# Block-sorted attention with a gated MLP: half of the first q by another queue, spatial weights turned in pairs, single output tiles, and a new order of units

## The chip, the cores and the metric

The kernel runs on one core of a Trainium2 chip. The metric is the device time of one execution in microseconds (us), the median of several runs. A profiled execution stands beside them: its span runs from the first to the last instruction of the core, and its own time is a little longer than the span.

## What is computed

The inputs are q, k and v (batch 4, 8 heads, 768 tokens, head size 64), an 8 x 8 matrix `sort_net` for each batch and head, and the weights of the MLP. All are fp32, and so is the output, 4 x 768 x 512. Cut to what matters:

```python
P = sort_net
for _ in range(5):                       # Sinkhorn rounds
    P = exp(P - max(P, -1)); P = P / sum(P, -1); P = P / sum(P, -2)
k_sorted = einsum('bhij,bhjcd->bhicd', P, k_blocks)      # 8 blocks of 96 tokens
v_sorted = einsum('bhij,bhjcd->bhicd', P, v_blocks)
attn = softmax(q_block @ k_sorted_block.T / 8)           # within each block
x = (attn @ v_sorted_block) as [batch, token, 512]
h = relu(x @ w_in);  u, v = h[..., :512], h[..., 512:]
v_n = (v - mean(v)) / sqrt(var(v) + 1e-6)                # over the 512 features
v_s = einsum('ts,bsd->btd', w_spatial, v_n) + b_spatial  # over the 768 tokens
out = (u * v_s) @ w_out
```

## The kernel before, in words

The work is written as units, short functions named by two letters. The string ORDER (lines 18 to 50) lists 355 of them by hand; the loop at line 755 calls them one after the other. No scheduler moves anything: each engine (and each engine's DMA queue) gets its instructions in the order in which the units issue them, and starts each one as soon as those before it on that engine have started and what it needs is there. In an item such as `SC:1:0:3:0` the first number of a unit that uses TensorE is the PSUM tile (four tiles of two banks, `ps0` to `ps3`); a letter A, D or P names ScalarE, VectorE or GpSimd; then come batch, head pair (four per batch) or tile, and half.

**Preamble.** `S0` loads sort_net by SyncE (L183). `SK:0` to `SK:4` (L224) are the Sinkhorn rounds: an exp on ScalarE (L232), then six short VectorE steps, strictly one after the other. `ID` makes the identity matrix on GpSimd, `MC` (L210) spreads it over 512 columns, `MA` and `MB` (L204, L207) make a mask. `DM` units (L217) are dummy matmuls on zeros. `PR` (L247) brings the Sinkhorn result to all partitions; `P0` (L261) multiplies it with the mask into the sorting matrices of batch 0 on VectorE, `PC` (L270) copies it to SBUF for `PD` (L273), which does the same for the other batches on GpSimd.

**Loads.** `L` (L157) issues all big loads on GpSimd's DMA queue, which casts from fp32 to bf16 on the way. q, k and v of a batch take one `ld` slot of 768 KB each. There are eight such slots, used in turn by q, k, v, the two halves of w_spatial and, later, the output tiles; a load waits until its slot is free. In order of issue: q0, k0, v0, v1, k1, q1, w_in's v half (`wv`), its u half (`wu`), the first half of w_spatial (`wsa`), and so on.

**Attention of a batch.** `QT` (one head pair, L312) and `QQ` (two, L318) turn q on TensorE (L308) and copy it out of PSUM. `KT` (L371) multiplies k with the sorting matrix. For batch 0, `VT` and `VB` (L374, L377) do the same for v. For batches 1 to 3, `VM` (L387) sorts v for all heads, and `VC` (L401, the DMA at L404) lets SyncE's queue copy each of the eight blocks of 96 tokens into `vb`, where `IV` has set a column of ones (L215). `SC` (L415) makes the scores and their exp (L428); `AT` (L460) multiplies with v and divides by the sum on VectorE (L476, L477). `XT` (L492) turns the result on TensorE; for batches 2 and 3 `XD` (L483) does it by a transposing DMA of SyncE's queue.

**MLP of a batch.** `VP` (L528, matmuls L535) is the v half of the first projection, with its relu; `ST`, `LN`, `LA` (L546 to L568) normalise on VectorE and ScalarE; `UP` (L570) is the u half (L578). `WT` (L502) turns one of the six 128-row strips of w_spatial (six transposes and one 768-wide copy). `SP` (L585) multiplies with the spatial weights and adds the bias, `GT` (L602) multiplies with u on GpSimd or VectorE. `OP` (L609) makes two output tiles of 128 tokens at once (eight matmuls, L616), `OE` (L623) copies them out of PSUM, and `OS` (L629) stores them by SyncE's queue. For the last batch there are finer units: `SH` and `GH` (L641, L654) work on tokens 0 to 511 or 512 to 767, and `OH`, `OI`, `OJ` (L661, L671, L676) make, copy and store one output tile or half of one.

`CK` and `CF` (L680, L695) test that sums stayed in range, `LF` (L701) loads the flag into all engines; the general path behind the branch at L759 is not taken.

Of the kernel before, what the change touches and what calls it, by code (L numbers as in the profile page):

```python
# [23 lines left out]
VM:3:A:1:3 AT:2:0:0:0 IV:1 VB:0:D:0:3 L:v:3:0:8 SC:1:0:3:0 VC:1:4:8 AT:2:0:2:0 SC:3:0:2:1 AT:0:0:3:0 BI SC:1:0:3:1
KT:2:A:1:3 AT:3:0:0:1 XT:1:A:0:0:2 AT:0:0:3:1 XT:2:A:0:0:0 XT:3:D:0:1:0 VC:1:0:4 KT:1:A:1:1 QQ:0:D:1:2 KT:2:A:1:0
PD:2:4:8 KT:3:A:1:2 QQ:1:A:1:0 AT:0:0:2:1 VP:2:D:0:0:1 SC:3:1:3:1 XT:0:D:0:1:2 VP:1:D:0:2 SC:3:1:0:1 ST:0:2 ST:0:0
SC:2:1:1:0 VP:0:A:0:4:5 VP:1:A:0:3 ST:0:1 ST:0:5 ST:0:3 SC:3:1:1:1 ST:0:4 SC:2:1:2:1 UP:0:A:0:1:0 UP:3:A:0:0:1
AT:1:1:1:1 L:k:3:0:8 AT:2:1:3:1 LN:0:0:6 PD:3:4:8 L:q:3:0:8 PD:3:0:4 UP:0:A:0:1:1 LA:0:1 AT:1:1:0:1 LA:0:0
UP:3:A:0:0:0 LA:0:5 WT:2:A:0 LA:0:2 WT:0:D:5 LA:0:3 WT:1:A:1 WT:3:D:4 WT:0:D:2 SC:2:1:3:0 AT:3:1:2:1 VM:1:A:2:1
WT:0:D:3 LA:0:4 VM:2:A:2:3 SC:3:1:0:0 VM:1:A:2:0 VM:0:D:2:2 VC:2:4:8 SP:2:0:3 AT:3:1:1:0 VC:2:0:4 AT:0:1:3:0 GT:D:0:3  # L30
SP:1:0:1 SP:2:0:2 SC:0:1:2:0 AT:1:1:0:0 KT:3:A:2:3 GT:P:0:2 XT:2:A:1:1:2 KT:0:D:2:1 KT:3:A:2:0 QQ:1:D:2:0 GT:P:0:1
QQ:2:D:2:2 KT:0:A:2:2 AT:3:1:2:0 SP:1:0:0 SC:3:2:0:0 XT:0:D:1:1:0 XT:2:A:1:0:0 XT:1:D:1:0:2 AT:3:2:0:0 SC:0:2:1:0
VM:2:A:3:2 VP:1:A:1:2:3 GT:P:0:0 VM:0:A:3:3 AT:2:2:1:0 ST:1:3 VP:3:D:1:4:5 VM:0:A:3:0 VM:2:D:3:1 VP:1:A:1:0:1
SC:0:2:3:0 SC:2:2:0:1 ST:1:5 OP:3:0:2 ST:1:0 ST:1:4 OE:A:0:2 VC:3:4:8 ST:1:2 SC:0:2:3:1 SC:1:2:1:1 UP:2:A:1:1:0
UP:3:A:1:0:1 VC:3:0:4 ST:1:1 AT:1:2:3:0 UP:0:D:1:0:0 LN:1:0:6 LA:1:3 LA:1:1 SC:3:2:2:1 SC:1:2:2:0 OP:2:0:0 KT:1:D:3:1
OE:A:0:0 KT:3:A:3:2 QQ:0:A:3:2 OS:0:2 LA:1:2 AT:2:2:2:0 LA:1:5 LA:1:0 LA:1:4 AT:1:2:3:1 OP:3:0:4 XD:2:0 AT:0:2:0:1
OE:A:0:4 UP:2:A:1:1:1 AT:3:2:1:1 AT:1:2:2:1 XD:2:1 SP:0:1:0 SC:1:3:2:0 QQ:2:D:3:0 KT:3:D:3:3 GT:P:1:0 KT:0:A:3:0
VP:1:D:2:0:1 SC:2:3:0:1 SC:3:3:1:0 VP:0:A:2:4:5 AT:3:3:2:0 AT:1:3:0:1 ST:2:4 SP:2:1:2 ST:2:1 ST:2:0 GT:P:1:2
SC:3:3:0:0 SC:1:3:3:1 VP:0:A:2:2:3 AT:2:3:1:0 ST:2:2 SP:1:1:3 SC:2:3:3:0 ST:2:5 GT:P:1:3 SC:0:3:2:1 SP:3:1:1 ST:2:3
SC:0:3:1:1 AT:2:3:0:0 UP:1:A:2:1:1 AT:0:3:3:0 LN:2:0:6 GT:P:1:1 UP:3:A:2:0:1 UP:1:A:2:1:0 LA:2:1 AT:2:3:3:1 AT:0:3:1:1  # L40
OP:3:1:2 AT:2:3:2:1 LA:2:3 OE:A:1:2 LA:2:2 UP:0:A:2:0:0 OP:2:1:0 LA:2:5 LA:2:0 OP:0:1:4 XD:3:0 XD:3:1 LA:2:4 OE:A:1:4
CK OE:D:1:0 SP:3:2:3 GT:P:2:3 CF:0 SP:2:2:2 VP:0:A:3:0:1 VP:1:D:3:2:3 VP:3:A:3:4:5 ST:3:2 ST:3:5 OS:0:4 SP:2:2:0
ST:3:1 SP:3:2:1 GT:P:2:0 UP:0:A:3:0:1 GT:D:2:2 ST:3:3 UP:2:A:3:0:0 UP:3:A:3:1:0 ST:3:4 ST:3:0 LN:3:0:6 LF LA:3:0
# [21 lines left out]
def kernel(  # L65
# [38 lines left out]
    def ps_tile(n, dt=FP32):  # L104
        return psum.tile([128, 2, 512 if dt == FP32 else 1024], dt, name=f"ps{n}", tag=f"ps{n}")

    def copy(eng, out, in_):
        if eng == "A":
            nc.scalar.copy(out=out, in_=in_)  # L109
# [39 lines left out]
    st = {}  # L149
    count = {"e": 0, "k": 0}  # L150

    def ld_tile(name):
# [55 lines left out]
        nc.vector.tensor_copy(out=mask16, in_=m32)  # L208

    def u_MC():  # L210
        nc.vector.tensor_copy(out=spread, in_=ident[0:BH, 0:BH].to_broadcast([BH, BH, TB]))
# [579 lines left out]
```

## Time and profile before

| | |
|---|---|
| median of 3 runs | 161.76 us (161.35 to 162.33) |
| the profiled execution | 162.01 us |
| its span | 160.1 us, mean granted TensorE clock 0.985 |
| DMA, bytes | GpSimd's queue 12.19 MB, SyncE's queue 10.70 MB |
| exp of the scores, L428, ScalarE | 32 of 810 ns, 24.5 us |
| spatial matmuls, L590 | 144 of 326 ns, 25.1 us |

Busy times are sums of instruction durations with overlaps counted once; matmuls are pipelined, so a matmul of 326 ns starts well before the one ahead of it has ended. "Granted clock" is the share of TensorE's full clock that it was given. SPq and POOLq are the sequencers of SyncE and GpSimd as issuers of DMAs. In a group row, the part behind the last bar is the time in which the engine stood idle before these instructions, with what ended it.

### The profile page before, as it was taken

Reading aid. Unit: us, or ns where it says so; the run is one execution under the profiler, and the core shown is the slowest. Engines: PE = TensorE matmul, PEld = TensorE weight load, DVE = VectorE, ACT = ScalarE, POOL = GpSimd, SP = SyncE. Lnnn points to the kernel's source line nnn. Section 1 sums busy time; section 2 is a strip of 40 time slices with the busy share of each in tenths; the row PEclk is TensorE's granted clock in tenths of the full one; section 3 lists DMA queues with packets and bytes.
Section 4 is the critical chain, followed back from the end, with each engine's and each line's share of the span. In section 5 each row is a group of like instructions: output and inputs, shape, how many; then the busy total and the mean of one; then the engine's idle time right before and its main releaser. Section 6 shows DMA issues by size and latency. Waiting matters only on the chain.

```text
span 160.1 us, 3999 instructions
## 1 busy us (share of the span) xinstructions
...
## 2 busy tenths in 40 slices
...
GB/s 14 184 204 205 204 205 204 207 217 249 264 206 205 213 248 220 204 130 108 184 49 98 100 5 0 0 4 98 122 107 209 57 0 0 0 330 327 39 315 55
DMA packets 27526, 23.19 MB, mean 145 GB/s; under 512 B 7280, under 2 KB 24432, under 8 KB 27504
## 3 DMA queue, kind: packets, MB, share of 16 engines
q0 software_dynamic: 14864, 12.19, 48.5%
q1 hardware_dynamic: 12640, 10.70, 23.7%
...
## 4 chain that ended last, share of the span: by engine, by line
PE 76%; DVE 8%; ACT 6%; DMA 4%; issue 1%
PE ps L590 14%; PE ps L578 13%; PE ps L535 12%; PE ps L616 12%; PE ps L646 5%; PE ps L469 4%; PE ps L423 3%; PE ps L364 3%; DMA xT<-x_sb 3%; PE ps L391 2%; PE ps L499 2%; ACT kt L109 2%; PE ps L308 2%; ACT ex L428 2%; DVE x_sb L477 2%; PE ps L505 1%
## 5 line engine op out<-in xcount | busy, mean ns | idle before, releaser
L606 POOL TENSOR_TENSOR gt<-z,u_sb 128x768 bf16<-128x768 f32 x10 | 17.0, 1706 | 76.1 <-ACT ex L428 42.2
L428 ACT ACTIVATE ex<-ps 96x768 bf16<-96x768 f32 x32 | 24.5, 810 | 18.0 <-PE ps L423 17.9
L590 PE MATMUL ps<-wspT,v_sb 128*128 128x384 bf16 x144 | 25.1, 326 | 0.0
L535 PE MATMUL ps<-w_in_sb,xT 128*128 128x512 bf16 x96 | 22.4, 379 | 0.9 <-ACT kt L109 0.8
L477 DVE TENSOR_TENSOR x_sb<-ps,rec_all 96x512 bf16<-96x512 f32 x32 | 22.0, 686 | 1.1
L578 PE MATMUL ps<-xT,w_in_sb 128*128 128x384 bf16 x128 | 22.6, 326 | 0.0
L616 PE MATMUL ps<-w_out_sb,gt 128*128 128x512 bf16 x88 | 20.2, 379 | 0.0
L109 ACT COPY o_sb<-ps 128x1024 f32<-128x1024 f32 (+1 forms) x9 | 8.4, 943 | 20.5 <-PE ps L616 19.8
L590 PEld LDWEIGHTS <-v_sb 128*128 128x128 bf16 x144 | 13.6, 98 | 8.7
L552 DVE BATCH_NORM_STATS2 stats<-v_sb 128x6 f32<-128x512 bf16 x24 | 16.2, 676 | 1.3 <-ACT v_sb L115 1.1
L115 ACT ACTIVATE u_sb<-ps 128x768 bf16<-128x768 f32 x14 | 11.4, 814 | 9.6 <-PE ps L578 9.5
L578 PEld LDWEIGHTS <-w_in_sb 128*128 128x128 bf16 x128 | 11.8, 98 | 7.4
L596 DVE TENSOR_TENSOR z<-ps,b_bc 128x768 f32<-128x768 f32 x12 | 11.5, 955 | 5.5 <-PE ps L590 4.0
L535 PEld LDWEIGHTS <-xT 128*128 128x128 bf16 x96 | 8.9, 98 | 10.8 <-issue 0.9
L616 PEld LDWEIGHTS <-gt 128*128 128x128 bf16 x88 | 8.3, 98 | 9.2
L115 ACT ACTIVATE v_sb<-ps 128x1024 bf16<-128x1024 f32 (+1 forms) x8 | 7.7, 969 | 10.7 <-PE ps L535 10.7
L476 DVE RECIPROCAL rec_all<-ps 96x8 f32<-96x8 f32 x32 | 6.3, 196 | 8.6 <-PE ps L469 8.4
L469 PE MATMUL ps<-vb,ex 96*128 96x65 bf16 x256 | 12.1, 193 | 0.3 <-DVE x_sb L477 0.2
L469 PEld LDWEIGHTS <-ex 96*128 96x128 bf16 x256 | 10.3, 97 | 3.6 <-DVE x_sb L477 0.4
L220 PE MATMUL ps<-warm 128*128 128x512 bf16 x36 | 9.8, 442 | 1.3 <-DVE warm L193 1.3
L423 PE MATMUL ps<-qT,kt 64*128 64x96 bf16 x256 | 9.6, 205 | 0.3 <-ACT kt L109 0.3
L423 PEld LDWEIGHTS <-kt 64*128 64x128 bf16 x256 | 6.2, 94 | 6.3 <-issue 3.8
...
## 6 DMA issues: line engine op xcount, KB each, us to landing
...
```

What stands on the lines that cost most here:

```text
L109: nc.scalar.copy(out=out, in_=in_)
L115: nc.scalar.activation(out=out, in_=in_, func=AF.Relu)
L423: nc.tensor.matmul(t[:, hh, 0:HW].rearrange("p (g x) -> p g x", g=G)[:, :, ii * TB:(ii + 1) * TB], lhsT=kT[rows, i * BLK:i * BLK + 128], r ...
L428: nc.scalar.activation(out=e_tile(b, hp, ih).rearrange("p h (x g) -> p h x g", g=G), in_=t[0:BLK, :, 0:HW].rearrange("p h (g x) -> p h x g ...
L469: nc.tensor.matmul(t[:, hh, ii * VW:ii * VW + D + 1], lhsT=e[:, c:c + 128], rhs=vb[b % 2][:, ih * NI + ii, 2 * hp + hh, 0:D + 1], start=Tr ...
L477: nc.vector.tensor_mul(out=x_sb[:, hp].rearrange("p i (h d) -> p h i d", h=2), in0=tv[:, :, :, 0:D], in1=_raw_ap(rec, 0, [rec.ap[0], [NI, ...
L535: nc.tensor.matmul(t[:, x, :], lhsT=st["xT", b][:, n // 3, kc, (n % 3) * 128:(n % 3 + 1) * 128], rhs=w_in_sb[:, kc, DH:DFF], start=(kc == ...
L552: nc.vector.bn_stats(out=stats, in_=st["v_sb", b, n])
L578: nc.tensor.matmul(t[:, x, 0:HW], lhsT=w_in_sb[:, kc, mc * 128:(mc + 1) * 128], rhs=st["xT", b][:, ih, kc, :], start=(kc == 0), stop=(kc = ...
L590: nc.tensor.matmul(t[:, x, 0:HW], lhsT=st["v_sb", b, n][:, mc * 128:(mc + 1) * 128], rhs=wspT[:, 3 * x:3 * x + 3, n, :], start=(n == 0), s ...
L606: eng.tensor_mul(out=gt, in0=st["z", b, mc], in1=st["u", b, mc // 2][:, mc % 2])
L616: nc.tensor.matmul(t[:, x, :], lhsT=st["gt", b, mc][:, (n0 + x) * 128:(n0 + x + 1) * 128], rhs=w_out_sb[:, mc, :], start=(mc == 0), stop=( ...
```

## The change

1. Half of the first q. Heads 0 to 3 of batch 0's q come by a new unit `LH` on SyncE's queue, as fp32, into an `ld` slot of their own; a new unit `QC` casts them on ScalarE, two heads each, into the bf16 tile. GpSimd's queue loads heads 4 to 7 only, as its first DMA. `QC:A:0` stands ahead of the fourth Sinkhorn round, `QC:A:1` ahead of the fifth.
2. `MC` goes from VectorE to ScalarE, `PC` from ScalarE to VectorE.
3. `WW`, a function that was there but not used, turns two strips of w_spatial in one unit, with one 1536-wide copy: three such units instead of six `WT`. The second half of w_spatial is loaded ahead of the first.
4. Output. Tiles 0 to 3 of the last batch, two `OP` units before, become single `OH` tiles as well: seven `OH`, `OI`, `OJ` instead of three, nine `OP` and `OE` instead of eleven, ten `OS` instead of fifteen.
5. ORDER is new throughout. All four q turns of batch 0 come ahead of `PR`, six of the 36 dummies behind it. `IV:1` comes ahead of q2's load. The first output store, `OS:1:2`, stands behind `XD:3:0` in SyncE's order, while `OS:0:2` stood ahead of all `XD`.

The functions:

```diff
     def u_MC():
-        nc.vector.tensor_copy(out=spread, in_=ident[0:BH, 0:BH].to_broadcast([BH, BH, TB]))
+        nc.scalar.copy(out=spread, in_=ident[0:BH, 0:BH].to_broadcast([BH, BH, TB]))
...
+    def u_LH(eng, half):
+        half = int(half)
+        lo = half * H // 2
+        st["q32", half] = t = ld.tile([128, H // 2, G * D], FP32, name="q32", tag="ld")
+        (nc.scalar if eng == "A" else nc.sync).dma_start(
+            out=t, in_=_raw_ap(q, lo * S * D, [[G * D, 128], [S * D, H // 2], [1, G * D]]))
+
+    def u_QC(eng, hp):
+        hp = int(hp)
+        if ("q", 0) not in st:
+            st["q", 0] = ld_tile("q_in")
+        copy(eng, st["q", 0][:, 2 * hp:2 * hp + 2], st["q32", hp // 2][:, 2 * (hp % 2):2 * (hp % 2) + 2])
```

The function that replaces `WT`:

```python
    def u_WW(ps, eng, c):
        t = ps_tile(ps, BF16)[:, :, 0:S]
        for x in range(2):
            for n in range(G):
                nc.tensor.transpose(
                    t[:, x, n * 128:(n + 1) * 128],
                    st["ws", (int(c) + x) // (G // 2)][:, (int(c) + x) % (G // 2), n * 128:(n + 1) * 128], ident)
        copy(eng, wspT[:, int(c):int(c) + 2].rearrange("p c n t -> p c (n t)"), t)
```

ORDER, the start, the attention of batch 0 up to the first projection, and the end:

```diff
-S0 CO L:q:0:0:8 SK:0 L:k:0:0:8 ID SK:1 DM:1:6:512 DM:2:6:512 SK:2 MC L:v:0:0:8 DM:0:6:512 MA L:v:1:0:8 IV:0 L:k:1:0:8
-SK:3 L:q:1:0:8 DM:1:6:512 DM:3:6:512 DM:2:6:512 SK:4 QT:1:A:0:0 PR:2 MB QT:0:A:0:3 P0:6:8 P0:4:6 L:wv L:wu L:wsa
-P0:2:4 P0:0:2 QT:3:D:0:1 PC:A KT:1:A:0:1 KT:0:A:0:0 BH PD:1:4:8 L:wsb QT:3:D:0:2 IV:2 KT:2:D:0:2 SC:1:0:1:1 L:v:2:0:8
...
+S0 CO SK:0 LH:S:0 SK:1 L:q:0:4:8 ID SK:2 L:k:0:0:8 L:v:0:0:8 MC QC:A:0 MA SK:3 DM:1:6:512 IV:2 L:v:1:0:8 L:k:1:0:8
+DM:0:6:512 L:q:1:0:8 IV:0 QC:A:1 SK:4 DM:3:6:512 MB L:wv QT:2:A:0:0 DM:1:6:512 L:wu DM:3:6:512 QT:2:D:0:1 QT:3:A:0:3
+QT:1:A:0:2 PR:0 P0:0:2 P0:4:6 P0:6:8 L:wsb P0:2:4 L:wsa L:v:2:0:8 DM:2:6:512 PC:D KT:3:A:0:3 KT:2:D:0:1 KT:1:A:0:0
+PD:1:4:8 VT:0:D:0:0 VT:3:A:0:1 KT:1:D:0:2 PD:1:0:4 SC:2:0:3:0 L:k:2:0:8 VB:0:D:0:0 VB:3:D:0:1 VT:2:A:0:3 VT:1:D:0:2
+PD:2:4:8 SC:0:0:0:1 IV:1 SC:3:0:1:0 VB:2:D:0:3 PD:2:0:4 VM:1:A:1:1 L:q:2:0:8 AT:0:0:0:1 SC:3:0:2:0 VB:2:D:0:2
+SC:0:0:2:1 AT:1:0:3:0 SC:2:0:0:0 AT:3:0:1:0 VM:0:A:1:0 SC:1:0:1:1 AT:2:0:2:0 AT:3:0:0:0 KT:0:A:1:0 KT:1:A:1:3
+AT:2:0:2:1 SC:3:0:3:1 XT:0:D:0:0:2 XT:1:A:0:0:0 AT:2:0:1:1 BH VM:3:A:1:2 VM:0:A:1:3 L:q:3:0:8 AT:1:0:3:1 QQ:2:D:1:0
+KT:3:A:1:2 XT:1:A:0:1:2 XT:0:A:0:1:0 KT:2:A:1:1 QQ:3:D:1:2 VP:1:A:0:0:1 SC:0:1:0:1 ST:0:1 SC:2:1:1:1 ST:0:0 VP:3:A:0:2
+L:v:3:0:8 VC:1:4:8 VP:1:A:0:4:5 ST:0:2 VP:0:D:0:3 SC:2:1:3:1 ST:0:3 SC:3:1:3:0 UP:1:A:0:1:1 SC:2:1:1:0 ST:0:4
+AT:3:1:1:1 UP:0:A:0:0:1 ST:0:5 LN:0:0:6 AT:1:1:0:1 LA:0:2 LA:0:1 LA:0:4 LA:0:5 LA:0:3 SC:3:1:2:1 UP:2:A:0:0:0 WW:1:A:4
...
+AT:1:3:3:1 OP:3:1:4 OE:D:1:4 SC:0:3:1:1 SC:2:3:3:0 LA:2:0 OP:1:1:0 LA:2:1 LA:2:4 LA:2:5 AT:0:3:3:0 OP:3:1:2 OE:D:1:2
+XD:3:0 OE:A:1:0 UP:2:A:2:1:1 UP:1:A:2:1:0 LA:2:2 LA:2:3 AT:3:3:1:1 SP:2:2:1 SC:1:3:2:1 SC:0:3:0:1 SP:3:2:3 AT:0:3:0:1
+VP:1:A:3:0:1 OS:1:2 OS:0:2 AT:3:3:2:1 CK SP:0:2:2 ST:3:0 XD:3:1 UP:1:A:3:0:0 GT:D:2:1 CF:2 SP:3:2:0 VP:0:A:3:2:3
...
-SH:2:3:2:1 OP:3:3:0 GH:P:3:1:1 OE:D:3:0 GH:P:3:2:1 OP:2:3:2 GH:P:3:3:1 OH:3:3:5:0:256:0:4 OI:D:3:5:0:256 OE:A:3:2
-OS:3:0 OH:1:3:4:0:512:0:4 OJ:3:5:0:256 OI:D:3:4:0:512 OS:3:2 OH:2:3:5:256:512:0:4 OI:A:3:5:256:512 OJ:3:4:0:512
-OJ:3:5:256:512
+SH:3:3:0:0 GH:D:3:0:0 SH:0:3:0:1 OS:2:2 SH:1:3:1:1 GH:P:3:1:1 SH:2:3:3:1 OH:3:3:2:0:512:0:4 GH:D:3:0:1 OS:2:0:0:1
+OS:2:0:1:2 OH:1:3:3:0:512:0:4 GH:P:3:3:1 OI:A:3:2:0:512 OI:A:3:3:0:512 OJ:3:2:0:512 OH:2:3:5:0:256:0:4 OJ:3:3:0:512
+OH:0:3:5:256:512:0:4 OI:D:3:5:0:256 OH:3:3:1:0:512:0:4 OH:2:3:0:0:512:0:4 OI:A:3:1:0:512 OJ:3:5:0:256
+OH:1:3:4:0:512:0:4 OI:D:3:0:0:512 OI:D:3:5:256:512 OI:A:3:4:0:512 OJ:3:1:0:512 OJ:3:5:256:512 OJ:3:4:0:512
+OJ:3:0:0:512
```

More of the change, by code (lines that the diff above doesn't have):

```diff
@@ L24 @@
[L24 to L43, printed above, removed]
@@ new lines @@
+VC:1:0:4 XT:3:D:1:1:0 PD:3:4:8 AT:0:1:2:1 WW:2:D:0 WW:3:A:2 L:k:3:0:8 AT:1:1:3:1 LA:0:0 UP:0:A:0:1:0 PD:3:0:4
+VM:2:D:2:1 BI VM:3:A:2:2 XT:1:D:1:1:2 L:wo SC:0:1:2:0 SC:2:1:0:0 VM:3:A:2:0 SP:1:0:0 AT:2:1:3:0 VM:0:A:2:3
+VP:3:A:1:4:5 AT:0:1:2:0 AT:2:1:0:0 SP:1:0:2 AT:2:1:1:0 SP:0:0:3 KT:3:A:2:2 XT:2:D:1:0:0 XT:1:A:1:0:2 GT:P:0:2
+KT:0:A:2:3 GT:P:0:3 ST:1:5 KT:3:D:2:0 QQ:2:A:2:0 QQ:1:D:2:2 ST:1:4 KT:0:A:2:1 VP:3:D:1:0:1 GT:D:0:0 ST:1:1 SC:2:2:2:1
+SC:1:2:2:0 SP:0:0:1 VC:2:0:4 VC:2:4:8 SC:1:2:0:0 SC:3:2:3:1 VP:2:A:1:2:3 AT:3:2:2:1 UP:1:A:1:1:1 VM:2:A:3:3 ST:1:0
```

14 lines of the change are left out of this document (9 added, 5 removed).

## The prediction

> **What bounds the kernel now.** First the page: the span, and what the DMA engines move in each fortieth (4.0 us) of it.
>
> ```profile
> span 160.1 us, 3999 instructions
> GB/s 14 184 204 205 204 205 204 207 217 249 264 206 205 213 248 220 204 130 108 184 49 98 100 5 0 0 4 98 122 107 209 57 0 0 0 330 327 39 315 55
> ```
>
> Then the busy times by stretch, which show where the 11 us without TensorE lie.
>
> ```profile
> 11.60:32.40 20.80, 18.55 (x428) 14.71 (x429) 16.84 (x34) 18.96 (x26) 8.40 (x11) 1.00 1.30 205
> 32.40:153.00 120.60, 120.30 (x1185) 70.66 (x1184) 90.73 (x186) 59.38 (x79) 27.09 (x21) 1.00 0.63 135
> 153.00:160.10 7.10, 0.00 (x0) 0.00 (x0) 0.33 (x1) 0.37 (x1) 0.00 (x0) 0.66 0.47 159
> ```
>
> The columns after the length are PE, PEld, DVE, ACT, POOL. From 32.4 to 153.0 TensorE is busy 120.30 of 120.60 us: a new order cannot gain there, only open holes. Whatever can be won lies before 32.4 and in the 7.1 us behind the last matmul. In the middle stretch ScalarE is at 18.96 of 20.80, 91%. Third, the chain of work, at the joints of these stages.
>
> ```profile
> 7.61 0.34 DVE spread L211
> 11.69 0.36 PE ps L250 x8
> 31.89 0.60 issue
> 32.48 1.89 PE ps L535 x8
> 153.02 0.37 ACT o_sb L109
> ```
>
> Until 11.69 the Sinkhorn rounds set the pace. The first projection (L535, it needs w_v) starts at 32.48. What holds it are the loads, as the timeline (start, duration) and the issue-to-landing times of the q, v and w_v rows show.
>
> ```profile
> 1.26 1.06 POOL L163 DMA_DIRECT2D q_in<-in_q_dram  x1 [0.81 <-POOLq L775]
> 3.72 1.77 POOL L163 DMA_DIRECT2D v_in<-in_v_dram  x2
> 7.34 0.91 POOL L168 DMA_DIRECT2D w_in_sb<-in_moe_w_in_dram  x1
> 16.51 0.36 PEld L364 LDWEIGHTS <-v_in 128*64 128x64 bf16 x12
> DMA to landing us min/median/max: 7.4/7.4/7.4
> DMA to landing us min/median/max: 12.7/14.6/16.5
> DMA to landing us min/median/max: 24.0/24.0/24.0
> ```
>
> q of batch 0 lands at 1.26 + 7.4 = 8.7, v at 3.72 + 12.7 = 16.4 and is used at 16.51, w_v at 7.34 + 24.0 = 31.3 and is used at 32.48. GpSimd's queue moves 204 GB/s without a pause, so each load waits for those before it; but its first slice moves only 14 GB/s, because it starts late.
>
> **The change, part by part.** Preamble, as the timeline, the DMA issues and the chain have it now:
>
> ```profile
> 0.74 0.41 SPq L183 DMA_DIRECT2D p_all<-in_sort_net_dram  x1
> 1.28 9.82 PE L220 MATMUL ps<-warm 128*128 128x512 bf16 x36 [1.28 <-DVE warm L193]
> 5.10 5.51 PEld L220 LDWEIGHTS <-warm 128*128 128x128 bf16 x26 [0.28 <-issue]
> 5.88 0.26 ACT L232 ACTIVATE p_all<-p_all 32x64 f32<-32x64 f32 x1 [1.50 <-DVE p_all L243]
> 7.64 0.26 ACT L232 ACTIVATE p_all<-p_all 32x64 f32<-32x64 f32 x1 [1.50 <-DVE p_all L243]
> 11.97 0.86 PE L308 MATMUL ps<-ident,q_in 128*64 128x128 bf16 x24
> L115 ACT ACTIVATE v_sb<-ps 128x512 bf16<-128x512 f32 x1 | 0.6, 592 | 0.0
> L109 ACT CAST kt<-ps 128x768 bf16<-128x768 f32 x11 | 8.6, 799 | 1.9 <-PE ps L364 1.9
> 150.81 0.38 SPq L631 DMA_DIRECT2D out_dram<-o_sb  x1
> DMA to landing us min/median/max: 2.8/2.8/2.8
> ```
>
> MC goes from VectorE to ScalarE and takes 0.34 off the Sinkhorn chain. ScalarE now has, between the exp that ends at 6.14 and the one due at 7.64, MC (0.59, as the 512-wide row) and the cast QC:A:0 (0.80, as the 768-wide row): 1.39 in a gap of 1.50. That holds if the fp32 half is there by 6.75. A load of this kind is not in the trace. It is issued at 0.74 + 0.41 = 1.15. From below: 512 KB written on SyncE's empty queue (issue at 150.81) landed in 2.8, so 4.0; 768 KB adds 256 KB at 330 GB/s, 0.8, so 4.8. From above: the 9.1 us of a block copy of 99 KB under load (row below) and the other bytes, 2.0 at 330, so 12.3. I take 5, by the row of the empty queue, since the other queue hardly moves before 4. Queued behind QC:A:0 on ScalarE are the fourth and fifth exp, QC:A:1 and the copies of the q turns; VectorE's Sinkhorn steps wait for the exps. TensorE: 10 dummies by 5.10, 8 more at 5.51 / 26 = 0.212 to 6.8, a wait for the cast to 7.6, one turn (half of 0.86) to 8.0, 12 dummies to 10.6, three turns to 11.9. PR is thus 0.2 later than 11.69, though p_t is 0.3 earlier; the six dummies placed behind PR lie under P0, and no q turn is left between the first k turns. PC moves behind P0 on VectorE, where it still releases PD, and with it GpSimd's later loads, within 0.3 of now; the loads queued on the DMA cover that. Sum **0** (-0.3 to +0.5).
>
> Loads: GpSimd's queue carries half a q less ahead of all others: 384 KB at 204 GB/s, 1.9 us. Against it the DMA engines carry the half as fp32, at 330 GB/s (the slices of output writes) 2.4 us, of which those up to about 4.2 fall into a time in which they are idle. So all later loads come between 0 (fp32 counted by its written bytes at 204 GB/s, 3.9 us from 2.2 on, then the other half: q at 8.0 as now) and 1.9 us earlier; I take 1.5, nearer to the rate of the row with SyncE's fp32 packets. Up to the first projection the new order issues the same units as the old, only one turn of xT more. ScalarE's part of them gets shorter (one QQ, one VB and PC go, one VM and one XT come), VectorE had 4 us spare there. So the first projection starts at 32.48 - 1.5 = 31.0: **-1.5**. The xT turn done earlier is 0.4 less afterwards: **-0.4**.
>
> ```profile
> 57.67 0.47 PE ps L499 x8
> ```
>
> The Trainium skill, "Trainium Kernel Development and Optimization", Key Constraints, says against this that the queues of SyncE, ScalarE and GpSimd run on the same 16 DMA engines, and that issuing from several saves only the issue time. By it alone the loads gain about half of an issue, and the sum would be 1.0 smaller; the first slice's 14 GB/s speaks for more.
>
> The stretch without holes: what the new order can lose. The vb blocks of batch 1 are the nearest case. Their landings (the first four, the second four), what SyncE waited for, how long it takes to issue eight of them, and TensorE's pieces:
>
> ```profile
> DMA to landing us min/median/max: 7.0/7.3/7.8
> DMA to landing us min/median/max: 7.3/8.9/9.1
> SPq L404 <- POOL vb L215: 6.4, 1, 6.4
> 71.77 5.50 SPq L404 DMA_DIRECT2D vb<-vm  x8
> 120.53 5.18 PE ps L535 x24
> 105.08 1.30 PE ps L578 x8
> 97.47 0.45 PE ps L423 x16
> xT<-x_sb SPq DMA_TRANSPOSE x4, 3.8
> ```
>
> Now the blocks wait 6.4 us for a memset (IV:1) on GpSimd. The new order has it far ahead, so SyncE issues VC:1:4:8 when the last VM of batch 1 is copied. One AT, two QQ, two KT and two XT, an estimated 3.3 of TensorE less 0.9 for the copy, lie between it and the first projection: first issue 28.6, the fourth three times 0.69 later at 30.7, landed 7.6 later at 38.3. AT:3:1:1:1 is due after 24 matmuls of L535, five SC and one UP: 31.0 + 5.18 + 1.1 + 1.3 = 38.6. Margin 0.3; with 9.1 it is a hole of 0.8. In batch 3, XD:3:1 (3.8 and two VectorE steps) has two SP and one UP, 5.2 us, for cover. I put **+0.4** for holes (0 to 2). Behind a late AT stand all TensorE's later units.
>
> Pairs: three wide copies for six. Two ScalarE copies of 0.8 become two of 1.5, VectorE's four become one.
>
> ```profile
> L109 ACT COPY wspT<-ps 128x768 bf16<-128x768 bf16 x2 | 1.5, 806 | 0.0
> L109 ACT COPY qT<-ps 128x1536 bf16<-128x1536 bf16 x2 | 2.9, 1458 | 0.0
> ```
>
> The cover is the projections around them; ScalarE is at 59.38 of 120.60 in this stretch. **0**; without cover 1.3. The extra ld slot that q32 takes shifts every later slot by one; the tiles that must then be free are turned or stored long before: 0. The output stores of batches 0 to 2, which go out later, are through some 4 us before the last tiles: 0.
>
> The end. The last issue of before and its landing:
>
> ```profile
> L678 SPq DMA_DIRECT2D out_dram<-o_sb x1: 1759/1759/1759, 154.0 to 154.0; - x1
> DMA to landing us min/median/max: 4.4/4.4/4.4
> ```
>
> Batch 3's 1.5 MB are written behind 150.81, most of it queued in the last 2 us, so the last store lands 4.4 after its issue, at 158.4, and 1.7 later the span ends. Now seven tiles leave one by one, the first ready 4.3 before TensorE ends. At the end E of the last matmul, one copy of 0.6 and two issues of 0.4 remain, the last at E + 1.1. If its landing takes 2.7 (512 KB on an empty queue took 2.8), the span ends at E + 5.5 instead of E + 7.1: **-1.6**. Bounds: 0 with 4.4 as now; -2.4 with 1.9.
>
> Sum: 0 - 1.5 - 0.4 + 0.4 - 1.6 = -3.1. The profiled execution took 162.01 with a span of 160.1, 0.25 above the median of 161.76; so 158.9 against itself and **158.7** against the median.
>
> **The rivals.**
> A. The loads come hardly earlier (only issue time is saved): the first projection moves by 0.5 instead of 1.5; 159.7. For it: all queues share engines. Against it: the 14 GB/s.
> B. The wait moves to the vb blocks or to a transposing DMA: holes of 2 instead of 0.4; 160.3. For it: a margin of 0.3 us. Against it: the memset no longer holds the blocks.
> C. The last stores queue as before, 4.4 behind the last issue; 160.3. For it: seven issues of 0.4 on one queue. Against it: over half of the bytes are off before E.
> D. **Slower**: the fp32 half comes late and stands in ScalarE's queue ahead of the fourth exp. If it lands at the upper bound, 12.3, the exp starts at 13.1 instead of 7.64, 5.5 late, and so does PR, on which every k turn hangs. From PR to the first projection the engines need what they need now at ScalarE's 91%, about 19.3, so the loads no longer pace it: 5.5 more than forecast, 164.2. It decides from a landing at about 10 on (6.8 and the 3.1 that are won); between 6.8 and 10 it only eats the gain. Against it: SyncE's queue is empty, and GpSimd's hardly runs before 4.
> That the loads or the end do not do what they are for is A and C.
>
> **How the numbers follow.** Forecast 0.50, A 0.13, B 0.16, C 0.11, D 0.10. The range goes from 157.5 (loads 1.9, no holes, end 2.0) to 161.8, where two of the rivals A to C come together (1.5 for no gain in the loads, 1.6 for none at the end); D and a rest are left out. About 0.5% is what a measurement can tell from no change (161.0 to 162.6). Faster: forecast, A, and most of B and C, 0.79; same 0.10, from B and C with further losses and mild D; slower 0.11.
>
> **What would show it.** Right: q32 landing by 6.8 and the fourth exp within 0.2 of 7.64; v and w_v landing some 1.5 earlier; the first L535 at about 31; TensorE without a pause behind it; the span ending 5.5 after the last matmul. Wrong: ScalarE idle ahead of the cast while the exps wait; TensorE waiting for vb or xT; landings above 4 us at the end.

## The result and the profile after

The changed kernel takes 161.42 us (median of 20 runs, 161.17 to 161.81); the kernel before took 161.97 beside it (20 runs, 161.35 to 162.5). The ratio is 0.9968, 95% interval 0.9956 to 0.9979: a third of a per cent faster, where 2% was forecast. The profiled execution took 161.53, its span went from 160.1 to 159.7.

First the page and the busy times by the stretches of before (columns PE, PEld, DVE, ACT, POOL, then granted clock, DMA share, GB/s).

```profile
span 159.7 us, 3977 instructions
q8 instruction: 14, 0.23, 0.6%
```

```profile
11.60:32.40 20.80, 18.90 (x414) 14.66 (x410) 16.56 (x32) 17.42 (x24) 9.46 (x11) 1.00 1.30 205
32.40:153.00 120.60, 118.07 (x1169) 69.85 (x1179) 88.08 (x181) 62.43 (x83) 24.18 (x19) 1.00 0.62 135
153.00:160.00 7.00, 0.67 (x4) 0.10 (x1) 0.86 (x2) 0.59 (x1) 0.00 (x0) 0.89 0.38 136
```

ScalarE has 1.5 us less to do between 11.6 and 32.4 (less was forecast, without a figure), yet TensorE has not come further at 32.4. Behind it, TensorE now has holes and works on until 153.7. (The records of 14 of its 1661 matmuls are missing from this trace, so its 118.07 is somewhat too low.)

The front, from the timeline (start, duration) and the issue-to-landing times. The landing of the fp32 half comes first, then that of k and v of batch 0 together, then that of w_v.

```profile
1.22 0.42 SPq L343 DMA_DIRECT2D q<-in_q_dram  x1
3.63 0.88 POOL L164 DMA_DIRECT2D v_in<-in_v_dram  x1
7.37 0.79 POOL L169 DMA_DIRECT2D w_in_sb<-in_moe_w_in_dram  x1
6.60 0.82 ACT L110 CAST q_in<-q 128x768 bf16<-128x768 f32 x1
7.70 0.26 ACT L233 ACTIVATE p_all<-p_all 32x64 f32<-32x64 f32 x1 [0.27 <-DVE p_all L244]
```

```profile
DMA to landing us min/median/max: 4.6/4.6/4.6
DMA to landing us min/median/max: 8.8/10.3/11.8
DMA to landing us min/median/max: 23.0/23.0/23.0
```

The fp32 half is there at 5.8 and the fourth exp runs at 7.70, 0.06 later than before. v lands at 3.63 + 11.8 = 15.4 (before 16.4) and w_v at 30.4 (31.3): the loads are 1.0 earlier. TensorE makes nothing of it:

```profile
11.76 0.36 PE L251 MATMUL ps<-p_t,spread 32*128 32x32 bf16 x8
15.45 0.86 PE L378 MATMUL ps<-pd,v_in 128*64 128x128 bf16 x24 [0.80 <-DMA v_in<-in_v_dram]
32.26 0.38 PE L309 MATMUL ps<-ident,q_in 128*64 128x128 bf16 x7 [0.22 <-issue]
32.57 0.39 PE L549 MATMUL ps<-w_in_sb,xT 128*128 128x512 bf16 x1
```

In the new order it waits 0.80 for v, which it did not do before, it pauses again at 32 in the middle of a q turn with no releaser named ("issue"), and the first projection starts at 32.57 (before 32.48).

TensorE has two large holes, at 137.5 and at 147.4. For the first, the row of `LF`'s load on VectorE, and the timeline behind it:

```profile
L716 DVEq TENSOR_LOAD <-flag x1: 1171/1171/1171, 132.8 to 132.8; - x1
```

```profile
136.63 0.30 ACT L572 ACTIVATE rstd<-mv,eps 128x6 f32<-128x6 f32 x1 [3.48 <-DVE mv L567]
137.08 0.99 ACT L110 COPY o_sb<-ps 128x1024 f32<-128x1024 f32 x1
138.12 1.46 PE L592 MATMUL ps<-xT,w_in_sb 128*128 128x384 bf16 x8 [0.64 <-ACT o_sb L110]
```

For the second, VectorE's product `gt`, the weight loads of the single output tiles that need it, and the matmuls ahead of them:

```profile
145.25 2.13 PE L660 MATMUL ps<-wspT,v_sb 128*128 128x256 bf16 x18
147.32 0.69 DVE L673 TENSOR_TENSOR gt<-z,u_sb 128x512 bf16<-128x512 f32 x1
148.07 1.41 PEld L680 LDWEIGHTS <-gt 128*128 128x128 bf16 x8 [0.97 <-DVE gt L673]
```

TensorE has ended what stood ahead at 147.38 and goes on at 148.07, when `gt` is there: 0.69. The kernel before has no hole over 0.15 in all this stretch.

The end, by the last matmuls in the chain and the issues of the single stores:

```profile
150.36 3.32 PE ps L680 x17
```

```profile
L692 SPq DMA_DIRECT2D out_dram<-o_sb x7: 332/333/619, 149.8 to 155.4; - x7
DMA to landing us min/median/max: 2.0/2.4/2.7
```

TensorE ends at 153.68, the last store is issued at 155.4, and the span ends 6.1 behind TensorE (before 7.1). So of the 0.4 that the span lost, the first projection gives +0.1, TensorE's time from there to its end +0.6 (120.5 before, 121.1 now), and the end -1.0. The +0.6 is two holes of 1.3 together, and work that got shorter.

### The profile page after: what moved, and what is told of

The parts are those of the page before. It is cut to its first block, busy times and chain, and to the rows that moved or that the text cites. A ratio compares the mean times of both kernels' runs of the same rounds, so it can differ in the third digit from the quotient of the medians.

```text
span 159.7 us, 3977 instructions
## 1 busy us (share of the span) xinstructions
PE 147.6 (92%) x1647; PEld 89.2 (56%) x1661; DVE 113.1 (71%) x261; ACT 85.7 (54%) x117; POOL 42.2 (26%) x46
## 5 line engine op out<-in xcount | busy, mean ns | idle before, releaser
L620 POOL TENSOR_TENSOR gt<-z,u_sb 128x768 bf16<-128x768 f32 x10 | 16.4, 1642 | 76.1 <-DVE rec_all L490 55.1
L592 PE MATMUL ps<-xT,w_in_sb 128*128 128x384 bf16 x128 | 23.3, 326 | 0.6 <-ACT o_sb L110 0.6
L549 PE MATMUL ps<-w_in_sb,xT 128*128 128x512 bf16 x88 | 21.6, 379 | 0.5 <-issue 0.2
L116 ACT ACTIVATE u_sb<-ps 128x768 bf16<-128x768 f32 x15 | 12.2, 812 | 10.8 <-PE ps L592 7.9
L116 ACT ACTIVATE v_sb<-ps 128x1024 bf16<-128x1024 f32 (+1 forms) x10 | 9.8, 982 | 14.4 <-PE ps L549 14.4
L592 PEld LDWEIGHTS <-w_in_sb 128*128 128x128 bf16 x128 | 11.8, 98 | 8.7 <-issue 0.9
L630 PE MATMUL ps<-w_out_sb,gt 128*128 128x512 bf16 x68 | 16.3, 379 | 0.2
L483 PEld LDWEIGHTS <-ex 96*128 96x128 bf16 x256 | 10.9, 97 | 3.8 <-DVE x_sb L491 0.3
L110 ACT CAST kt<-ps 128x768 bf16<-128x768 f32 x12 | 9.3, 804 | 5.9 <-PE ps L378 5.9
L630 PEld LDWEIGHTS <-gt 128*128 128x128 bf16 x72 | 6.6, 98 | 7.1
```

The costliest lines, as they stand in the source:

```text
L116: nc.scalar.activation(out=out, in_=in_, func=AF.Relu)
L483: nc.tensor.matmul(t[:, hh, ii * VW:ii * VW + D + 1], lhsT=e[:, c:c + 128], rhs=vb[b % 2][:, ih * NI + ii, 2 * hp + hh, 0:D + 1], start=Tr ...
L549: nc.tensor.matmul(t[:, x, :], lhsT=st["xT", b][:, n // 3, kc, (n % 3) * 128:(n % 3 + 1) * 128], rhs=w_in_sb[:, kc, DH:DFF], start=(kc == ...
L592: nc.tensor.matmul(t[:, x, 0:HW], lhsT=w_in_sb[:, kc, mc * 128:(mc + 1) * 128], rhs=st["xT", b][:, ih, kc, :], start=(kc == 0), stop=(kc = ...
L620: eng.tensor_mul(out=gt, in0=st["z", b, mc], in1=st["u", b, mc // 2][:, mc % 2])
L630: nc.tensor.matmul(t[:, x, :], lhsT=st["gt", b, mc][:, (n0 + x) * 128:(n0 + x + 1) * 128], rhs=w_out_sb[:, mc, :], start=(mc == 0), stop=( ...
```

## The experiments

Times are medians of runs beside the kernel before on the same chip, with the ratio to it. "First projection" is the start of the first matmul of `VP` in the profiled execution, "the end" the time from the last matmul to the span's end.

**The first four.** What the fp32 half and the order are worth, and the hole at 137.

no_fp32_half:

```diff
-S0 CO SK:0 LH:S:0 SK:1 L:q:0:4:8 ID
+S0 CO SK:0 SK:1 L:q:0:0:8 ID
-... MC QC:A:0 MA ... IV:0 QC:A:1 SK:4
+... MC MA ... IV:0 SK:4
```

> The changed kernel with all of the first q on GpSimd's queue again; the rest of its order kept. Theory 1 (TensorE stands at the first v turn until v of batch 0 lands, and all behind it follows): v lands 1.0 us later, at about 16.4, the first projection comes 0.8 to 1.0 later than 32.57, time about 162.3. Theory 2 (the engines' copies between 13 and 32 us set the pace and the loads do not): the first projection within 0.3 of 32.6, time 161.4 to 161.7. In both the fourth exp stays at 7.7, since nothing stands ahead of it on ScalarE but MC.

Measured: 162.2, ratio 1.0021 [1.0005, 1.0037]; first projection 33.68. The time is Theory 1's. But `PR` was late as well (12.87 instead of 11.76, since the first q turn waits for the whole q), so this run alone does not tell whether the loads or `PR` made the 1.1 by which the first projection is later.

old_order_fp32_half:

```diff
 (the ORDER of before)
-S0 CO L:q:0:0:8 SK:0
+S0 CO LH:S:0 L:q:0:4:8 SK:0
-MC ... SK:3
+MC QC:A:0 ... SK:3 QC:A:1
```

> The kernel before, with its own order, plus the fp32 half alone: q's heads 0 to 3 by SyncE, two casts and MC on ScalarE. Theory 1 (the loads pace the old order up to the first projection): loads 1.0 earlier, first projection at about 31.5 instead of 32.48, MC off VectorE's chain gives up to 0.25 more; time 160.7 to 161.1 against 161.97. Theory 2 (the engines set the pace): first projection within 0.3 of 32.48 less the 0.25 of MC, time 161.6 to 161.9.

Measured: 162.15, ratio 1.0019 [1.0000, 1.0038]; `PR` 12.12, first projection 32.55. Loads that come 1.0 earlier move nothing here, and Theory 1, the forecast's own reason, fails; so does Theory 2's time. But `PR` is 0.4 later than in the kernel before (11.68), because TensorE ends its dummies later, so this run alone does not clear the loads; old_order_fp32_early_pr and old_order_32_dummies below do that.

scores_ahead_of_v:

```diff
-PD:1:4:8 VT:0:D:0:0 VT:3:A:0:1 KT:1:D:0:2 PD:1:0:4 SC:2:0:3:0 L:k:2:0:8
+PD:1:4:8 KT:0:D:0:2 PD:1:0:4 SC:3:0:3:0 SC:2:0:0:1 SC:1:0:1:0 L:k:2:0:8 VT:0:D:0:0 VT:3:A:0:1
```

> The changed kernel with the last k turn and three score units of batch 0 put ahead of the first two v turns, as the kernel before had them. Theory 1 (the v turns ahead of the scores make TensorE and ScalarE idle until v lands): the first exp of scores at about 15.4 instead of 17.05, the first projection 0.7 to 1.2 earlier, time 160.3 to 160.8. Theory 2 (total work of the engines): first projection within 0.3 of 32.57, time 161.2 to 161.5.

Measured: 162.16, ratio 1.0024 [1.0007, 1.0041]; first projection 33.56. Theory 1 missed. Three exps run early, from 15.92, but the sorting of v on TensorE, at 15.45 and 18.05 in the changed kernel, now comes at 16.74 and 19.46, the fourth exp not before 23.13, and the first projection a microsecond later. What ScalarE won at first, the chain from v to `AT` lost. Part of that is again a later `PR` (12.28 for 11.76); how much, no run tells.

flag_behind_norm:

```diff
-GT:P:2:0 LF OS:0:0
+GT:P:2:0 OS:0:0
-LA:3:4 LA:3:3 SH:3:3:3:0
+LA:3:4 LA:3:3 LF SH:3:3:3:0
```

> The changed kernel with the load of the flag into the engines put behind the last normalisation of batch 3 instead of between two of its statistics. Theory 1 (the flag's 1.17 us on VectorE delay the statistics, the rstd on ScalarE, the copy behind it and so the matmuls at 138.1): the hole of 0.8 us at 137.1 closes, the last matmul ends 0.7 to 1.0 earlier, time 160.4 to 160.8. Theory 2 (the statistics are late anyway, by the relu of the last projection): hole and time within 0.2 of now, 161.2 to 161.6.

Measured: 160.54, ratio 0.9925 [0.9901, 0.9949]. TensorE goes from `OP` to `UP` without a pause (timeline, then the last matmuls in the chain):

```profile
131.90 5.34 PE L630 MATMUL ps<-w_out_sb,gt 128*128 128x512 bf16 x24
137.08 1.46 PE L592 MATMUL ps<-xT,w_in_sb 128*128 128x384 bf16 x8
```

```profile
149.32 3.32 PE ps L680 x17
```

So the hole came from one load of a flag. VectorE executes `LF` in its order, between the statistics of two tiles; it took 1.17 us there, `LN` on ScalarE waited 3.48 for the last statistics (here 2.27), and the copy behind `LN` is the one that frees the PSUM tile for `UP`. Here TensorE ends at 152.64; from the first projection at 32.33 that is 120.3. Against the changed kernel the medians give 0.9, the ratios 0.7.

The second hole stays:

```profile
147.03 5.60 PE L680 MATMUL ps<-w_out_sb,gt 128*128 128x512 bf16 x28 [0.69 <-DVE gt L673]
```

This trace has all 1661 matmuls. TensorE is busy for 119.47 of the 120.30 us, against 120.30 of 120.50 in the kernel before: its work got 0.8 shorter, and the hole takes 0.7 of that back. All ten kernels with the new order's end show it, 0.68 to 0.69; no run moved it.

**What paces the front.** In the new order, and with the other loads.

early_pr (and ps0 and ps2 exchanged in all items from `PR` on):

```diff
-QT:2:A:0:0 DM:1:6:512 L:wu DM:3:6:512 QT:2:D:0:1
+QT:2:A:0:0 DM:1:4:512 L:wu DM:3:4:512 QT:0:D:0:1
```

> The changed kernel with eight instead of twelve dummy matmuls behind the first q turn, and two PSUM tiles exchanged so that nothing else waits: PR, which TensorE reached at 11.76, can start when p_t is there, at about 11.45. Theory 1 (in the new order the landing of v of batch 0, at 15.4, paces what leads to the first projection): the first projection stays at 32.4 to 32.6, the time at that of the changed kernel, 161.4. Theory 2 (the chain of engine work from PR on paces it, as in the old order): everything from PR on comes 0.3 to 0.8 earlier, the first projection at 31.8 to 32.2, the time 160.7 to 161.1.

Measured: 161.43, ratio 0.9976 [0.9961, 0.9990], against 0.9968 for the changed kernel:

```profile
11.58 0.36 PE L251 MATMUL ps<-p_t,spread 32*128 32x32 bf16 x8
16.46 0.34 PE L437 MATMUL ps<-qT,kt 64*128 64x96 bf16 x8
```

`PR` is 0.2 earlier, the first scores (16.58 in the changed kernel) 0.1, the time is the same. Together with the 0.80 that TensorE waits for v, this is Theory 1: the new order is paced by v. The first projection at 32.22 alone would have spoken for Theory 2; but the kernel of the flag's run, with the same head as the changed one, shows 32.33, so a quarter of a us is what single executions differ by.

late_loads_early_pr (no_fp32_half, and):

```diff
-QT:2:A:0:0 DM:1:6:512 L:wu DM:3:6:512 QT:2:D:0:1
+QT:2:A:0:0 DM:1:6:512 L:wu QT:2:D:0:1
```

> The changed kernel without the fp32 half (GpSimd's queue loads the whole first q, so v of batch 0 lands at about 16.4 instead of 15.4), with six dummy matmuls fewer in front of PR, so that PR is not later than 11.9 although the first q turn is. Theory 1 (the landing of v paces the new order): the first projection at 33.4 to 33.7, as in the run without the fp32 half in which PR was late as well, time 162.1. Theory 2 (the chain from PR paces it): the first projection 20.8 behind PR, at about 32.6, time 161.3.

Measured: 162.08, ratio 1.0047 [1.0014, 1.0079]. The median is Theory 1's, with a reservation: of the 12 executions seven took 161.8 to 162.2 and five 163.4 to 163.7, and the profiled one (163.61) is of the five. In it, behind the longer wait for v, the granted clock was 0.81 (the last but two column) instead of the 1.00 of the changed kernel, so that the first projection (34.77) proves nothing about the loads:

```profile
16.59 0.86 PE L377 MATMUL ps<-pd,v_in 128*64 128x128 bf16 x24 [1.85 <-DMA v_in<-in_v_dram]
```

```profile
15.00:20.00 5.00, 3.30 (x60) 2.96 (x60) 2.92 (x4) 2.12 (x3) 2.90 (x3) 0.81 1.32 204
```

old_order_fp32_early_pr (old_order_fp32_half, and four dummies fewer):

```diff
-DM:1:6:512 DM:3:6:512 DM:2:6:512 SK:4
+DM:1:6:512 DM:3:6:512 DM:2:2:512 SK:4
```

> The order of before with the fp32 half on SyncE and its casts on ScalarE, and 32 instead of 36 dummy matmuls, so that PR can start when p_t is there. Theory 1 (loads pace the stage in the old order too): the first projection at 32.5 as in before, time 162. Theory 2 (in the old order the chain of engine work from PR paces it, while the loads land a microsecond before they are needed): PR at about 11.5, the first projection 20.4 behind it at 31.9, time 161.2 to 161.5.

Measured: 160.91, ratio 0.9942 [0.9922, 0.9962]; more than Theory 2 asked for.

```profile
11.59 0.36 PE L250 MATMUL ps<-p_t,spread 32*128 32x32 bf16 x8 [0.56 <-DVE mask L208]
31.13 1.89 PE L548 MATMUL ps<-w_in_sb,xT 128*128 128x512 bf16 x8
```

`PR` came 0.5 earlier than in old_order_fp32_half, the first projection 1.4. The other 0.9 is two pauses that are gone, 0.6 in front of the first projection and 0.3 at about 19.5. In the kernel before, TensorE's weight loads and the count of those up to 32.0 show the larger one (the second pair of numbers in the window row is PEld):

```profile
31.50 0.10 PEld L535 LDWEIGHTS <-xT 128*128 128x128 bf16 x1
32.49 0.53 PEld L535 LDWEIGHTS <-xT 128*128 128x128 bf16 x3 [0.89 <-issue]
```

```profile
0.00:32.00 32.00, 28.83 (x476) 18.98 (x477) 24.08 (x80) 21.12 (x32) 16.62 (x27) 1.00 1.16 178
```

The pause lies behind the 477th weight load. In old_order_fp32_half it lies behind the same one, 0.49 long; in the changed kernel, whose units there are others, behind the 478th, where no wait of the program stands:

```profile
31.97 0.10 PEld L548 LDWEIGHTS <-xT 128*128 128x128 bf16 x1
32.55 0.53 PEld L548 LDWEIGHTS <-xT 128*128 128x128 bf16 x3 [0.49 <-issue]
```

```profile
0.00:32.30 32.30, 29.35 (x476) 19.14 (x477) 23.72 (x78) 22.85 (x35) 17.60 (x28) 1.00 1.17 196
```

```profile
32.26 0.22 PEld L309 LDWEIGHTS <-q_in 128*64 128x64 bf16 x6 [0.38 <-issue]
```

```profile
0.00:32.00 32.00, 28.67 (x476) 19.07 (x478) 24.12 (x79) 22.28 (x34) 17.58 (x28) 1.00 1.17 196
```

The smaller pause stands 255 weight loads earlier in both orders, behind the 222nd and the 223rd. In the kernel before and in old_order_fp32_half:

```profile
19.35 0.11 PEld L364 LDWEIGHTS <-v_in 128*64 128x64 bf16 x2 [0.28 <-issue]
19.80 0.11 PEld L377 LDWEIGHTS <-v_in 128*64 128x64 bf16 x2 [0.29 <-issue]
```

A pause that stays at the same place in the instruction stream, whatever the instruction, points to the stream itself. The page has a queue for it: q8 brings 0.23 MB of instructions in 14 packets, 16 KB each. One of these starts at 30.04 in the kernel before, at 30.32 in old_order_fp32_half and at 29.82 in the changed kernel, and takes 0.94; TensorE goes on 2.45, 2.23 and 2.44 behind that start. Ahead of the smaller pause it is the same: packets at 17.01, 17.49 and 17.05, and TensorE goes on 2.3 behind each. Three more kernels pause in front of the first projection at the same count, no_fp32_half (0.57), flag_and_store_order (0.35) and last_tiles_in_pairs (0.21), and go on 2.3 to 2.5 behind their packets.

A rival is ScalarE's second cast of `kt`. In the kernel before it ends at 31.88, and the timeline names it as what ended TensorE's wait for the first matmul of the projection. But in old_order_fp32_early_pr and in old_order_fp32_same_count below, with the same units, that matmul starts 0.35 and 0.34 before this cast ends: it does not need it.

**Testing that.** The next four.

old_order_fp32_same_count (old_order_fp32_early_pr, with the four wide dummies replaced by four narrow ones):

```diff
-DM:2:2:512 SK:4
+DM:2:2:512 DM:2:4:8 SK:4
```

> The kernel old_order_fp32_early_pr (160.9, first projection at 31.1) with four dummy matmuls of 8 columns put in where four of 512 columns were left out, so that TensorE has as many instructions as in old_order_fp32_half while its time up to PR stays short. Theory 1 (TensorE's instructions come in packets of 16 KB; the one that is fetched at about 29.5 is not there before about 31.9, and in the old order its first instruction is the second matmul of the first projection): the pause returns, the first projection goes on at 31.8 to 32.1, the time 161.3 to 161.6. Theory 2 (the earlier PR alone brought the gain): no pause, first projection at 31.1, time 160.9.

Measured: 161.7, ratio 0.9991 [0.9978, 1.0005]:

```profile
31.48 0.10 PEld L548 LDWEIGHTS <-xT 128*128 128x128 bf16 x1
32.05 0.98 PEld L548 LDWEIGHTS <-xT 128*128 128x128 bf16 x6 [0.47 <-issue]
```

```profile
0.00:31.80 31.80, 29.08 (x477) 19.14 (x477) 23.69 (x78) 22.85 (x35) 17.14 (x27) 1.00 1.18 197
```

The pause is back, behind the 477th weight load and 2.24 behind the start of its packet, and the time is 0.8 longer for four matmuls of 8 columns: Theory 1, though 161.7 is 0.1 above its band. In the profiles TensorE ends 0.7 later: 0.2 is a later `PR` (11.81), 0.2 comes at the place of the smaller pause, and the rest from this one. Even the single instruction tells: TensorE's record has one semaphore instruction fewer ahead of the place than in old_order_fp32_half, and here the first matmul of the projection still runs, at 31.51, while there it stands behind the pause with the second weight load. The Trainium skill, "Runtime: NRT & Kernel Launch", Instruction fetch mechanics, says that an engine fetches its instructions by a DMA queue of its own in blocks of 16 KiB, and that crossing such a boundary is mostly hidden. The packets of 16 KB agree; here, in a stretch of short matmuls with all DMA engines busy, 0.4 to 0.9 us were not hidden.

old_order_32_dummies (the kernel before, without any fp32 half, and):

```diff
-DM:1:6:512 DM:3:6:512 DM:2:6:512 SK:4
+DM:1:6:512 DM:3:6:512 DM:2:2:512 SK:4
```

> The kernel before, without the fp32 half, with 32 instead of 36 dummy matmuls; nothing else. Theory 1 (in the old order the loads have a microsecond in hand, and what the run old_order_fp32_early_pr won came from PR and from the place of TensorE's instruction packets): PR at about 11.5, the first projection at 31.1 to 31.6 (w_v lands at 31.3 here), time 160.9 to 161.2, so that the fp32 half itself is worth 0 to 0.3. Theory 2 (the fp32 half brought it by its earlier loads): first projection at 32 or later, time 161.6 or more.

Measured: 161.32, ratio 0.9968 [0.9952, 0.9983]. Four dummies fewer bring what the whole change brought. The chain of waits names what comes next:

```profile
7.34 24.39 DMA w_in_sb<-in_moe_w_in_dram
31.73 0.05 issue
31.77 0.39 PE ps L535
```

With the pause moved away, the landing of w_v does hold the first projection, at 31.77; with the fp32 half it is 31.13 and the time 0.4 shorter (160.91). Neither theory had it exactly: in the old order the half is worth something only once the pauses are gone.

new_order_12_fewer (early_pr, flag_and_store_order, and):

```diff
-SK:4 DM:3:6:512 ... PR:2 ... L:v:2:0:8 DM:0:6:512 PC:D
+SK:4 DM:3:4:512 ... PR:2 ... L:v:2:0:8 PC:D
```

> The changed kernel with the flag behind the last normalisation, the store of tile 0 first, and twelve dummy matmuls fewer (four ahead of PR, six behind it, two in the first group), so that the 16 KB instruction packet that TensorE waited for in front of the first projection begins inside the projection. Theory 1 (in the new order the landing of v paces the stage, and the packet costs at most 0.4): first projection at 31.9 to 32.2, time 160.0 to 160.3 against 160.4 of the kernel with flag and store moved. Theory 2 (the stage is held by TensorE's instruction packets here too): first projection at 31.3 or earlier, time 159.5 or less.

Measured: 160.89, ratio 0.9949 [0.9920, 0.9978]; first projection 33.42. Both theories missed. The missing dummies left TensorE idle, and in the profiled execution (161.49; the 12 lie between 160.24 and 162.6) the clock was 0.66 between 15 and 20:

```profile
13.19 1.20 PE L378 MATMUL ps<-pd,k_in 128*64 128x128 bf16 x36 [1.27 <-DVE pd L265]
15.56 1.49 PE L378 MATMUL ps<-pd,v_in 128*64 128x128 bf16 x24 [1.18 <-DMA v_in<-in_v_dram]
```

```profile
15.00:20.00 5.00, 4.44 (x84) 4.05 (x84) 2.96 (x5) 1.95 (x4) 3.06 (x3) 0.66 1.31 204
```

How much the packet costs in the new order thus stays open here; it is at most its pauses, 0.38 in front of the first projection and 0.17 at 19.3. It is probably little: in early_pr, where the same place falls elsewhere among the units, TensorE pauses for 0.14, and the time is that of the changed kernel.

old_head_new_rest (the ORDER of old_order_fp32_early_pr up to the first projection, behind it that of flag_and_store_order with the PSUM tiles renumbered; the loads and `VC` stay in the places of the old head):

```diff
 ... AT:0:0:2:1
-VP:2:D:0:0:1 SC:3:1:3:1 XT:0:D:0:1:2 VP:1:D:0:2 ...
+VP:2:A:0:0:1 XT:1:D:0:1:2 SC:0:1:0:1 ST:0:1 SC:3:1:1:1 ST:0:0 VP:1:A:0:2 ...
```

> The order of before up to the first projection, with the fp32 half and 32 dummies; from there the order of the changed kernel (pairs, single last tiles), the flag's load behind the last normalisation and the store of tile 0 ahead of those that wait. Theory 1 (the new order's loss at the front and the flag's load hide the gain at the end): first projection at 31.1, no hole, last matmul at about 151.4, span end 6.0 behind it at 157.4, time 158.8 to 159.4, close to what was forecast for the change. Theory 2 (the parts are not additive, the rest of the new order needs the head of its own): holes of 1 or more behind the first projection, time 160 or more.

Measured: 160.16, ratio 0.9894 [0.9878, 0.9910], the lowest median of all, though its interval overlaps those of old_order_single_stores, flag_behind_norm and flag_and_store_order; first projection 31.16, the end 5.8. It is 0.8 above Theory 1's band and inside Theory 2's: from the first projection to TensorE's end it takes 121.05, against 120.3 in flag_and_store_order. The parts do not simply add up, but the version beats both kernels.

**The end.** flag_and_store_order (flag_behind_norm and):

```diff
-OJ:3:1:0:512 OJ:3:5:256:512 OJ:3:4:0:512 OJ:3:0:0:512
+OJ:3:1:0:512 OJ:3:0:0:512 OJ:3:5:256:512 OJ:3:4:0:512
```

> The changed kernel with the flag's load behind the last normalisation (as in the run of that alone, 160.5) and the store of the last-but-one finished tile (tile 0 of batch 3) put ahead of the two issues that wait for later copies; nothing else moves. Theory 1 (the end behind the last matmul is longer than forecast because the last issue in SyncE's queue is that of a tile which has long been ready, behind two issues that wait): the last issue at 1.1 instead of 1.7 behind the last matmul, the span's end 0.5 to 0.9 earlier, 159.7 to 160.0. Theory 2 (the landing of the bytes that are queued sets the end, whatever the order of issues): no change against the flag's run, 160.5.

Measured: 160.44, ratio 0.9906 [0.9878, 0.9934], the end 6.0 as without the edit, the last issue at 154.7, still 1.8 behind the last matmul. Theory 1 falls: the order of issues is not the reason. The last-but-one issue again takes 0.6 instead of 0.33 and the last comes 0.5 behind it; what holds SyncE there stays open.

last_tiles_in_pairs (flag_behind_norm and):

```diff
-OH:3:3:2:0:512:0:4 ... OH:1:3:3:0:512:0:4 ... OI:A:3:2:0:512 OI:A:3:3:0:512 OJ:3:2:0:512 ... OJ:3:3:0:512
+OP:3:3:2 ... OE:A:3:2 ... OS:3:2
-OH:3:3:1:0:512:0:4 OH:2:3:0:0:512:0:4 OI:A:3:1:0:512 ... OI:D:3:0:0:512 ... OJ:3:1:0:512 ... OJ:3:0:0:512
+OP:2:3:0 ... OE:D:3:0 ... OS:3:0
```

> The changed kernel with the flag's load behind the last normalisation (160.5 with the last tiles one by one) and tiles 0 and 1, 2 and 3 of batch 3 again as pairs: one copy and one store of 512 KB each; tiles 4 and 5 stay single. Theory 1 (one by one is what shortened the end from 7.1 to 6.0 behind the last matmul): the end 7 or more behind the last matmul, the time 161.2 to 161.8. Theory 2 (the end got shorter because the new order finishes the first tiles earlier, not because they leave singly): the end at 6.0 to 6.3, the time 160.4 to 160.8.

Measured: 160.97, ratio 0.9946 [0.9929, 0.9963], the end 6.2. It lies between the two theories, nearer to Theory 2.

old_order_single_stores (old_order_fp32_early_pr and):

```diff
-OE:D:3:0 ... OE:A:3:2 OS:3:0 ... OJ:3:5:0:256 OI:D:3:4:0:512 OS:3:2
+OE:D:3:0:0:1 OE:D:3:0:1:2 OS:3:0:0:1 OS:3:0:1:2 ... OE:A:3:2:0:1 OE:A:3:2:1:2 ... OS:3:2:0:1 OS:3:2:1:2 OJ:3:5:0:256 OI:D:3:4:0:512
```

> The kernel old_order_fp32_early_pr (160.9, its span ends 7.8 behind the last matmul) with the copies and stores of tiles 0 to 3 of batch 3 split by tile and issued as each is copied; the matmuls and their order stay. Theory 1 (stores one by one are what shortens the end): the end 6.0 to 6.5 behind the last matmul, the time 159.3 to 159.8, the fastest so far. Theory 2 (the end goes with the order in which the tiles are finished): the end stays at 7.1 to 7.8, the time 160.6 to 161.

Measured: 160.43, ratio 0.9911 [0.9894, 0.9929], the end 7.0 instead of 7.8. This too lies between the theories, nearer to Theory 2. So single tiles bring 0.3 to 0.4 in the new order (against flag_behind_norm, by the ratios and by the medians) and 0.5 in the old. In the profiles they shorten the end by 0.2 and 0.8; but the 7.8 is from an execution of 161.4, 0.5 above its kernel's median, so the 0.8 is too much. In the new order the end went from 7.1 to 6.0. If single tiles make 0.2 of that, the rest would go with the order in which the tiles are finished; no run varied this by itself, so it is not shown.

## Why the prediction went wrong

- **What bounds the front: failed.** The step "What holds it are the loads" was wrong, and with it the term of -1.5, which measured +0.1. In the kernel before, w_v had landed at 31.3; TensorE then stood until 32.48 for its next 16 KB of instructions. The quoted chain row "31.89 0.60 issue" said so: the engine waited for nothing that the profile shows. Loads that came 1.0 earlier (forecast 1.5) could not shorten that. In the old order they counted only where the pauses had been moved (old_order_fp32_early_pr against old_order_32_dummies), 0.4.
- **"The new order issues the same units": true of the set, but not enough.** It turns v ahead of the first scores, and so waits 0.80 for v; early_pr leaves that as what paces it. In this order the earlier loads do count: without them the kernel takes 0.8 to 0.9 longer (no_fp32_half, with a later `PR` in it). The new order thus lost at the front about what the loads won.
- **Preamble, 0: right.** Landing at 5.8, before the 6.75 that was allowed; fourth exp at 7.70, `PR` at 11.76 (forecast 11.9).
- **One turn of xT less, -0.4: more than that.** Without holes, TensorE's work from the first projection to its end is 0.8 shorter (flag_behind_norm); where the other 0.4 comes from stays open.
- **Holes, +0.4: mis-sized, 1.3.** The vb blocks and the transposing DMAs, which the margins were reckoned for, made none. `LF`, which the diff moves between two statistics, made one of 0.64; its removal is worth 0.7 to 0.9. The other, 0.69, is the wait of the first single output tile for `gt`. Neither the load of the flag on VectorE nor this wait was in the prediction's list.
- **Pairs, 0: right** as far as the trace shows: there is no hole at the three `WW`. No run undid them.
- **The end, -1.6: mis-sized**, -1.0. The landings are as forecast (2.4, at most 2.7), the last issue is 0.7 later than forecast, and single tiles as such are worth 0.3 to 0.5.
- **Rivals.** A had the right place but the wrong cause: the loads came 1.0 earlier, not 0.5, and the first projection moved by nothing. B was right that TensorE would get holes (1.3), by waits that it did not name. C's queue did not form: the last store landed in 2.5, and what the end lost against the forecast lies in its later issue. D did not happen.

As terms: first projection +0.1 for -1.5, TensorE behind it +0.6 for 0, the end -1.0 for -1.6: -0.3 for -3.1, the span's change up to rounding.
